# Linear attention and SwiGLU on one core: chunks 0 and 1 as pairs of batches, tiled attention, eight PSUM banks in turn

## The chip, the core and the metric

The kernel runs on one core of a Trainium2 chip. The metric is the device time of one execution in microseconds (us). Three executions of the kernel before took 251.66, 251.06 and 250.78 us; their median is 251.06 us. Six units matter here: PE (TensorE, matmuls), DVE (VectorE), ACT (ScalarE), POOL (GpSimd[...]), SP (SyncE, which only issues DMAs here) and the DMA engines.

## What is computed

The inputs are q, k and v of shape (4 batches, 8 heads, 768 tokens, 64), two weight matrices of 512 x 1536, one of 1536 x 512, and a vector of 512. First comes a linear attention with a decay for each head, then an RMS norm over the 512 numbers of a token, then a SwiGLU network:

```python
for t in range(S):
    state = gamma[None, :, None, None] * state + np.einsum('bhd,bhe->bhde', k[:, :, t], v[:, :, t])
    y[:, :, t] = scale * np.einsum('bhd,bhde->bhe', q[:, :, t], state)
x = np.ascontiguousarray(y.transpose(0, 2, 1, 3)).reshape(B * S, H * D)
xn = x / np.sqrt(np.mean(x * x, axis=-1, keepdims=True) + 1e-06) * rms_g
g = xn @ w_gate
return (g / (1.0 + np.exp(-g)) * (xn @ w_val)) @ w_out
```

Both kernels take the 768 tokens in six chunks of 128. Within a chunk y is a masked (q k^T) v plus q times the state of the chunks before; then the state gains k^T v. The decay is folded into scales: v is multiplied by gamma^-position and y by gamma^position.

## The kernel before

A chunk has four units, one for each batch: 128 tokens on 128 partitions. For each chunk the network (`ffn`) then runs over all four batches together, 512 tokens wide. It has twelve `gv` steps (eight 128x512 matmuls each, one SiLU on ACT, one product hT on DVE) and a `down` for each batch (twelve 128x512 matmuls, one copy on ACT, one store). Chunk c's network is the outer loop, and the attention of chunk c+1 is laid between its steps by tables of slots (PLAN for chunks 2 to 5, PLAN1 for chunk 1). The schedule is manual: each engine executes its instructions in the order in which the code issues them, and waits where it needs another engine's result or a buffer.

A unit of attention has these pieces. `piece_t` transposes q and k on PE (chunks 0 and 1 only; from chunk 2 on a DMA issued on SP does it, in `cast`). `piece_a` computes a = k q^T for 8 heads into two PSUM tiles (eight matmuls that use 64 rows of the array each) and masks them on DVE (am, line 219). `piece_y` has eight matmuls am v (line 232), four with the state (line 237), four for k^T v (line 244), then on DVE the scaled copy x (line 247) and the state's sum st_f (line 259), on ACT the squares (line 251), on POOL mean and power (lines 272 and 275). `piece_n` scales x to xn, and `piece_x` (chunks 0 and 1) or a DMA turns xn over into xnT, which the network reads.

Chunk 0 has nothing to hide behind. A string of steps orders its four batches (line 384: C cast, T transpose, V scaled v, A, Y, W a quarter of the gate and value weights, N, X, S), and the network of chunk 0 starts when all four are done, after five matmuls whose result is not used (`warm_up`).

Loads: chunk 0's first batch and chunks 1 to 5 come as float32 by SP, in runs of 64 numbers (256 bytes), and POOL casts q and k to bf16 and scales v (lines 178 to 181). Batches 1 to 3 of chunk 0 and all weights come by POOL's queue, cast on the way.

PSUM has eight banks. Four belong to the pool `aps` (attention), four to `fps` (network, and chunk 0's k^T v); each pool hands out its four in turn.

```python
    aps = ctx.enter_context(tc.tile_pool(name="aps", bufs=4, space=bass.MemoryType.PSUM))
    fps = ctx.enter_context(tc.tile_pool(name="fps", bufs=4, space=bass.MemoryType.PSUM))
    PLAN = dict(cast=(0, 1, 2, 3), t=(1, 3, 5, 7), a=(4, 6, 8, 10), y=(6, 8, 10, 12), n=(8, 10, 12, 13), x=(8, 10, 12, 14))
```

Of the kernel before, what the change touches and what calls it, by code (L numbers as in the profile page):

```python
# [11 lines left out]
AX = mybir.AxisListType  # L12
# [5 lines left out]
def kernel(  # L18
# [11 lines left out]
    nc = tc.nc  # L30
# [15 lines left out]
    loads = ctx.enter_context(tc.tile_pool(name="loads", bufs=8))  # L46
    work = ctx.enter_context(tc.tile_pool(name="work", bufs=3))
    ffw = ctx.enter_context(tc.tile_pool(name="ffw", bufs=3))
    aps = ctx.enter_context(tc.tile_pool(name="aps", bufs=4, space=bass.MemoryType.PSUM))
    fps = ctx.enter_context(tc.tile_pool(name="fps", bufs=4, space=bass.MemoryType.PSUM))  # L50


    out_v = out.rearrange("(b c p) m -> c b p m", b=B, p=C)

    SYNC_DEP = mybir.DependencyInfo(mybir.DependencyClass.Sync, mybir.DependencyReason.DATA)


    raw = {}

    def load(c, b, after=None):  # L60
        t = []
        for name, src in (("q_f", q), ("k_f", k), ("v_f", v)):
            x = loads.tile([128, H, D], F32, name=name)
            i = nc.sync.dma_start(
                out=x, in_=src[b].rearrange("h (c p) d -> c p h d", p=C)[c])
            if after is not None:
                tc.add_manual_dep(i.ins, after.ins.name, SYNC_DEP, reason="transfer order")
            t.append(x)
        raw[c, b] = t

    raw0 = {}

    def load0(b):
        for name, src in (("qb", q), ("kb", k)):
            x = work.tile([128, DM], BF16, name=name, bufs=6)
            nc.gpsimd.dma_start(
                out=x.rearrange("p (h d) -> p h d", h=H),
                in_=src[b].rearrange("h (c p) d -> c p h d", p=C)[0])  # L80
            raw0[name, b] = x
        x = loads.tile([128, H, D], F32, name="v_f")
        nc.gpsimd.dma_start(out=x, in_=v[b].rearrange("h (c p) d -> c p h d", p=C)[0])
        raw0["v", b] = x

    load(0, 0)
    g_col = const.tile([128, KS], F32, name="g_col")
    with nc.allow_non_contiguous_dma(reason="one column per 128 entries"):
        nc.scalar.dma_start(out=g_col, in_=moe_rms_g.rearrange("(s p) -> p s", p=128))


    pos_i = const.tile([128, NCH], mybir.dt.int32, name="pos_i")
    nc.gpsimd.iota(pos_i, pattern=[[C, NCH]], base=1, channel_multiplier=1)

    lngs = const.tile([128, H], F32, name="lngs")
    for h in range(H):
# [5 lines left out]
    pos_f = const.tile([128, NCH], F32, name="pos_f")  # L102
    nc.vector.tensor_copy(pos_f, pos_i)
    darg = const.tile([128, NCH, H], F32, name="darg")
    nc.vector.tensor_tensor(
        out=darg, in0=pos_f[:, :, None].to_broadcast([128, NCH, H]),
        in1=lngs[:, None, :].to_broadcast([128, NCH, H]), op=ALU.mult)
    vdec = const.tile([128, NCH, H], F32, name="vdec")
    ydec = const.tile([128, NCH, H], F32, name="ydec")
    nc.scalar.activation(vdec, darg, AF.Exp, scale=-1.0, bias=zero)  # L110
    nc.scalar.activation(ydec, darg, AF.Exp, scale=1.0, bias=lnscale)

    warm = const.tile([128, 1], F32, name="warm")
    nc.scalar.activation(warm, zero, AF.Silu)
    mhalf = const.tile([128, 1], F32, name="mhalf")
    nc.vector.memset(mhalf, -0.5)
    ident = const.tile([128, 128], BF16, name="ident")
    make_identity(nc, ident)
    causal = const.tile([128, 128], BF16, name="causal")
    nc.gpsimd.memset(causal, 1.0)  # L120
    nc.gpsimd.affine_select(
        out=causal, in_=causal, compare_op=ALU.is_ge, fill=0.0, base=0,
        pattern=[[1, 128]], channel_multiplier=-1)
    for b in range(1, B):
        load0(b)

    g_bc = const.tile([128, DM], F32, name="g_bc")

    st_f = [const.tile([128, NHP, 2 * D], F32, name=f"st_f{b}") for b in range(B)]
    st_b = [const.tile([128, NHP, 2 * D], BF16, name=f"st_b{b}") for b in range(B)]
    for b in range(B):
        nc.vector.memset(st_b[b], 0.0)


    wg_b = const.tile([128, KS, DFF], BF16, name="wg_b")
    wv_b = const.tile([128, KS, DFF], BF16, name="wv_b")
    wo_b = const.tile([128, NFF, DM], BF16, name="wo_b")
    wg_v = moe_w_gate.rearrange("(k p) n -> p k n", p=128)  # L140
    wv_v = moe_w_val.rearrange("(k p) n -> p k n", p=128)
    wo_v = moe_w_out.rearrange("(n p) m -> p n m", p=128)
    WB = 384

    landed = {}

    def load_w(i):
        sl = slice(i * WB, (i + 1) * WB)
        nc.gpsimd.dma_start(out=wg_b[:, :, sl], in_=wg_v[:, :, sl])
        landed["w", i] = nc.gpsimd.dma_start(out=wv_b[:, :, sl], in_=wv_v[:, :, sl])  # L150

    def load_wo(i):
        sl = slice(i * 4, (i + 1) * 4)
        landed["wo", i] = nc.gpsimd.dma_start(out=wo_b[:, sl, :], in_=wo_v[:, sl, :])
# [296 lines left out]
```

## Time and profile before

| what | value |
|---|---|
| median of three executions | 251.06 us |
| span of the profiled execution, first to last instruction | 248.7 us |
| PE busy | 225.9 us, 91% of the span |
| DVE, ACT, POOL busy | 128.1, 87.4, 95.2 us |
| granted PE clock, mean | 0.993 |
| moved by DMA | 35.94 MB |
| DMA share in the 40 slices | near 90% or over in the first 15, little from slice 30 on |

The page gives busy times of each engine, and what ended its idle times. A busy PE says that matmuls were in flight; how fast they went is read from the distance of their starts. The median of the executions lies 2.4 us above the profiled span: that is time before the first and after the last instruction, or the difference of one execution from another.

### The profile page before, as it was taken

The page shows a single profiled execution, that of the slowest core. Times are in us where ns is not written, and L with a number is a line of the kernel's source. Part 1 is how long each engine was busy: PE and PEld are TensorE (multiplying, and loading weights), DVE is VectorE, ACT ScalarE, POOL GpSimd, SP SyncE. Part 2 cuts the span into 40 slices and gives each one's busy share as a digit, 9 for nine tenths or more (in the row PEclk, how much of TensorE's full clock was granted, in tenths as well). Part 3 has the DMA queues.
Part 4 walks back from the last instruction along what each step waited for, and adds up shares of the span by engine and source line. Part 5 has one row for each costly group of instructions (what it writes and reads, how often), then busy time and mean ns, then how long its engine had stood idle before and what let it go on. Part 6 is the DMA issues. An engine that isn't in the chain of part 4 may idle for free.

```text
span 248.7 us, 4121 instructions
## 1 busy us (share of the span) xinstructions
PE 225.9 (91%) x1495; PEld 114.4 (46%) x1521; DVE 128.1 (51%) x215; ACT 87.4 (35%) x170; POOL 95.2 (38%) x177
## 2 busy tenths in 40 slices
PE   1776999979996989999989999989999999999993
PEld 0553445545433545445544445544444444444443
DVE  4796337676234895036894046894047781134300
ACT  6365334531431242232342322433232422332221
POOL 8978144953850236910246910246900211000000
PEclk9997999999999999999999999999999999999999
DMA  9999999898997699955999356999453114200022
GB/s 140 174 195 203 196 219 221 151 199 167 218 290 109 144 222 189 229 127 87 213 209 175 127 131 98 199 207 209 122 115 66 21 21 129 86 0 0 0 87 86
DMA packets 108213, 35.94 MB, mean 145 GB/s; under 512 B 99040, under 2 KB 104928, under 8 KB 108192
## 3 DMA queue, kind: packets, MB, share of 16 engines
q1 hardware_dynamic: 95232, 29.24, 60.8%
q0 software_dynamic: 12288, 6.29, 19.0%
q8 instruction: 12, 0.20, 0.3%
q10 hardware_dynamic: 672, 0.13, 0.3%
q14 instruction: 9, 0.07, 0.1%
HBM read 28.58 MB, written 6.29 MB: 140 GB/s over the span
## 4 chain that ended last, share of the span: by engine, by line
PE 77%; DVE 10%; DMA 5%; issue 3%; ACT 3%; POOL 0%; SPq 0%; DVEq 0%; ACTq 0%
PE o_ps L361 24%; PE v_ps L338 21%; PE g_ps L335 21%; DVE am L219 4%; PE a_ps L215 3%; PE y_ps L232 2%; DMA v_f<-in_v_dram 2%; DVE x L247 2%; DMA k_f<-in_k_dram 2%; PE kv_ps L244 1%; PE y_ps L237 1%; DMA kT<-kb 1%; DVE xn L283 1%; PE o_ps L351 1%; PE qk_ps L199 1%
## 5 line engine op out<-in xcount | busy, mean ns | idle before, releaser
L341 DVE TENSOR_TENSOR hT<-sg,v_ps 128x512 bf16<-128x512 bf16 x72 | 49.4, 687 | 89.6 <-PE v_ps L338 83.2
L338 PE MATMUL v_ps<-xnT,wv_b 128*128 128x512 bf16 x282 | 73.4, 379 | 0.5
L335 PE MATMUL g_ps<-xnT,wg_b 128*128 128x512 bf16 x276 | 72.9, 380 | 0.4
L340 ACT ACTIVATE sg<-g_ps 128x512 bf16<-128x512 f32 x72 | 42.8, 594 | 63.7 <-PE g_ps L335 62.2
L361 PE MATMUL o_ps<-wo_b,hT 128*128 128x512 bf16 x269 | 60.8, 379 | 1.2 <-DMA wo_b<-in_moe_w_out_dram 0.8
L338 PEld LDWEIGHTS <-wv_b 128*128 128x128 bf16 x288 | 28.2, 98 | 34.0
L335 PEld LDWEIGHTS <-wg_b 128*128 128x128 bf16 x288 | 26.6, 98 | 31.5 <-issue 0.9
L361 PEld LDWEIGHTS <-hT 128*128 128x128 bf16 x276 | 26.6, 98 | 30.9 <-issue 0.8
L272 POOL TENSOR_SCALAR ms<-ssq 128x1 f32<-128x1 f32 x24 | 4.5, 189 | 92.4 <-ACT xsq L251 92.3
L251 ACT ACTIVATE xsq<-x 128x512 f32<-128x512 f32 x24 | 15.1, 630 | 48.7 <-DVE x L247 48.6
L219 DVE TENSOR_TENSOR am<-a_ps,causal 128x512 bf16<-128x512 f32 x48 | 30.8, 682 | 2.4 <-PE a_ps L215 2.4
L366 ACT COPY o_sb<-o_ps 128x512 f32<-128x512 f32 x23 | 13.5, 585 | 36.8 <-PE o_ps L361 30.7
L180 POOL TENSOR_TENSOR vp<-v_f,vdec 128x512 bf16<-128x512 f32 x20 | 20.7, 1037 | 3.4 <-DMA v_f<-in_v_dram 3.4
L268 POOL CAST st_b<-st_f 64x256 bf16<-64x256 f32 x40 | 17.3, 432 | 1.3
L247 DVE TENSOR_TENSOR x<-y_ps,ydec 128x512 f32<-128x512 f32 x24 | 16.4, 685 | 1.4 <-PE y_ps L237 0.8
L232 PE MATMUL y_ps<-vp,am 128*128 128x64 bf16 x192 | 12.0, 200 | 5.4 <-DVE am L219 5.1
L178 POOL CAST qb<-q_f 128x512 bf16<-128x512 f32 x20 | 12.1, 606 | 8.7 <-DMA q_f<-in_q_dram 7.9
L283 DVE SCALAR_TENSOR_TENSOR xn<-x,rstd,g_bc 128x512 bf16<-128x512 f32 x16 | 12.5, 784 | 5.5 <-POOL rstd L275 5.5
L232 PEld LDWEIGHTS <-am 128*128 128x128 bf16 x192 | 9.2, 101 | 13.1 <-DVE am L219 9.7
L275 POOL TENSOR_TENSOR rstd<-ms,mhalf 128x1 f32<-128x1 f32 x24 | 13.2, 552 | 2.0
L179 POOL CAST kb<-k_f 128x512 bf16<-128x512 f32 x20 | 12.2, 609 | 2.6 <-DMA k_f<-in_k_dram 1.7
L259 DVE TENSOR_TENSOR st_f<-st_f,kv_ps 128x512 f32<-128x512 f32 x16 | 10.8, 676 | 0.0
(60 smaller groups left out, 125.5 us busy)
## 6 DMA issues: line engine op xcount, KB each, us to landing
out_dram<-o_sb SPq DMA_DIRECT2D x23, 256.0 KB, 2.2
q_f<-in_q_dram SPq DMA_DIRECT2D x21, 256.0 KB, 4.8
k_f<-in_k_dram SPq DMA_DIRECT2D x21, 256.0 KB, 5.0
v_f<-in_v_dram SPq DMA_DIRECT2D x21, 256.0 KB, 5.1
wg_b<-in_moe_w_gate_dram POOLq DMA_DIRECT2D x4, 384.0 KB, 9.6
wv_b<-in_moe_w_val_dram POOLq DMA_DIRECT2D x4, 384.0 KB, 10.7
wo_b<-in_moe_w_out_dram POOLq DMA_DIRECT2D x3, 512.0 KB, 8.3
v_f<-in_v_dram POOLq DMA_DIRECT2D x3, 256.0 KB, 6.2
```

What stands on the lines that cost most here:

```text
L180: nc.gpsimd.tensor_tensor(out=vp, in0=v_f, in1=vdec[:, c, :, None].to_broadcast([128, H, D]), op=ALU.mult)
L219: nc.vector.tensor_tensor(out=am[:, i], in0=a_ps[i], in1=causal[:, None, :].to_broadcast([128, NHP, 128]), op=ALU.mult)
L232: nc.tensor.matmul(y_ps[:, h, :], d["am"][:, i, hp, :], d["vp"][:, h, :], start=first, stop=last, skip_group_check=True)
L247: nc.vector.tensor_tensor(out=x, in0=y_ps, in1=ydec[:, c, :, None].to_broadcast([128, H, D]), op=ALU.mult)
L251: nc.scalar.activation(xsq, x.rearrange("p h d -> p (h d)"), AF.Square, accum_out=ssq)
L268: nc.gpsimd.tensor_copy(st_b[b][r, :, i * 64:i * 64 + 64], st_f[b][r, :, i * 64:i * 64 + 64])
L283: nc.vector.scalar_tensor_tensor(out=xn, in0=x, scalar=d["rstd"], in1=g_bc, op0=ALU.mult, op1=ALU.mult)
L335: nc.tensor.matmul(g_ps, wg_b[:, s, sl], xnT[:, s, :], start=s == 0, stop=s == KS - 1)
L338: nc.tensor.matmul(v_ps, wv_b[:, s, sl], xnT[:, s, :], start=s == 0, stop=s == KS - 1)
L340: nc.scalar.activation(sg, g_ps, AF.Silu)
L341: nc.vector.tensor_tensor(out=hT[:, n, :], in0=sg, in1=v_ps, op=ALU.mult)
L361: nc.tensor.matmul(o_ps, hT[:, n, b * C:(b + 1) * C], wo_b[:, n, :], start=n == 0, stop=n == NFF - 1)
```

## The change

The body of the kernel is written anew; the arithmetic is the same.

- **Chunks 0 and 1 in pairs.** A unit is now a pair of batches: 64 partitions for each of two batches, two neighbouring tokens on a partition (e = 0, 1), loaded by `load_pair` in runs of 128 numbers (512 bytes). The pieces for a pair are `tp` (transposes), `ap` and `ap_mask`, `y0` or `y1`, `kvp`, and they use quarters or halves of the array. Chunk 0's decay goes into float32 masks (`mask_exp`), so that v needs only a cast, and y no scaling; its statistics are taken from PSUM, and its state comes later, from `vp_pair` on POOL and `kvp` on PE.
- **The network from two batches on.** Chunk 0's `gv` steps for feature blocks 0 to 4 run 256 tokens wide on the first pair, then on the second; blocks 5 to 11 run 512 wide. Chunk 1 does blocks 0 to 5 in halves.
- **One attention phase a pair** for chunks 2 to 5 (`phase`): a for the next pair, then y with the state, k^T v, and am v for two batches. The state is kept as 64 x 64 blocks, so that the state and k^T v matmuls are half as wide and use half the array each.
- **Eight PSUM tiles of one bank in turn** (`bank`), for everything.
- **Loads by POOL's queue**, q and k cast on the way; SP keeps the first pair's q and v and the second's v of chunk 0, and the transposing DMAs. POOL no longer casts q and k. Stores go from SP to ACT, but for the last half tile.
- Seven matmuls (`heat`) run at the start, and the SiLU table is loaded on ACT at the first SiLU instead of at the start.

The diff, cut to its core (the constants, the other pieces and most of the hand-written order are left out):

```diff
--- before.py
+++ after.py
-    loads = ctx.enter_context(tc.tile_pool(name="loads", bufs=8))
-    aps = ctx.enter_context(tc.tile_pool(name="aps", bufs=4, space=bass.MemoryType.PSUM))
-    fps = ctx.enter_context(tc.tile_pool(name="fps", bufs=4, space=bass.MemoryType.PSUM))
+    psum = ctx.enter_context(tc.tile_pool(name="psum", bufs=1, space=bass.MemoryType.PSUM))
...
+    pair_v = {n: s.rearrange("b h (c j e) d -> c b j h (e d)", c=NCH, e=2) for n, s in srcs.items()}
...
+    def bank(name, dtype=F32):
+        i = turn[0] % 8
+        turn[0] += 1
+        return psum.tile([128, 512 if dtype == F32 else 1024], dtype, name=name, tag=f"p{i}")
...
+    def load_pair(c, p, n, eng=None, f32=False, after=None):
+        u = U.setdefault((c, p), {})
+        if n == "v" or f32:
+            x = work.tile([128, H, 2 * D], F32, name=n + "2f", tag="x" if n == "q" else "v2f", bufs=2)
+        else:
+            x = work.tile([128, H, 2 * D], BF16, name=n + "2b", bufs=3)
+        for b in range(2):
+            i = (eng or nc.gpsimd).dma_start(out=x[b * 64:b * 64 + 64], in_=pair_v[n][c, 2 * p + b])
+            if after is not None:
+                tc.add_manual_dep(i.ins, after.ins.name, SYNC_DEP, reason="transfer order")
+        u[n] = x
...
+    def mask_exp(a):
+        for i in range(2):
+            for x in range(2):
+                nc.scalar.activation(mask0[a][i][:, x], reach, AF.Exp, scale=lng[2 * (2 * a + x) + i], bias=lnscale)
...
+    def heat(n):
+        hot = bank("hot")
+        for _ in range(n):
+            nc.tensor.matmul(hot, ones[:, :128], ones, start=True, stop=True)
...
+    def tp(c, p, n, a, eng):
+
+        u = U[c, p]
+        ps = bank("t_ps", BF16)
+        view = ps[:, :512].rearrange("p (x b e j) -> p x e b j", x=2, b=2, e=2)
+        for x in range(2):
+            for e in range(2):
+                for i in range(2):
+                    h = 2 * (2 * a + x) + i
+                    nc.tensor.transpose(view[i * 64:i * 64 + 64, x, e], u[n][:, h, e * D:e * D + D], ident)
+        t = work.tile([128, 2, 2, 2, 64], BF16, name=n + "2T", tag=n + "T", bufs=8)
+        copy(eng, t.rearrange("p x b e j -> p (x b e j)"), ps[:, :512])
+        u[n + "T", a] = t
...
+    def ap(c, p, a):
+        u = U[c, p]
+        qt, kt = u["qT", a], u["kT", a]
+        ps = [bank("a_ps") for _ in range(2)]
+        for x in range(2):
+            for e in range(2):
+                o = (x * 2 + e) * 128
+                for b in range(2):
+                    for i in range(2):
+                        r, t = slice(i * 64, i * 64 + 64), slice(b * 64, b * 64 + 64)
+                        nc.tensor.matmul(ps[i][t, o:o + 128], kt[r, x, b, e], qt[r, x, b], start=True, stop=True)
...
+        am = work.tile([128, 2, 2, 128], BF16, name="am2", tag="am", bufs=12)
+        m = mask0[a][i] if c == 0 else causal_p[:, None, :].to_broadcast([128, 2, 256])
+        last_mask[0] = nc.vector.tensor_tensor(
+            out=am.rearrange("p x e t -> p x (e t)"),
+            in0=u["a_ps", a][i].rearrange("p (x t) -> p x t", x=2), in1=m, op=ALU.mult)
...
+    def vp_pair(c, p):
+        u = U[c, p]
+        x = work.tile([128, H * 2, D], BF16, name="vp2", bufs=3)
+        nc.gpsimd.tensor_tensor(
+            out=x, in0=u["v"].rearrange("p h (e d) -> p (h e) d", e=2),
+            in1=vd_p[:, c].rearrange("p h e -> p (h e)")[:, :, None].to_broadcast([128, 2 * H, D]), op=ALU.mult)
...
+    def y0(p, a):
+        for x in range(2):
+            for i in range(2):
+                h = 2 * (2 * a + x) + i
+                for e in range(2):
+                    for b in range(2):
+                        r = slice(b * 64, b * 64 + 64)
+                        nc.tensor.matmul(u["y"][b][:, h * D:h * D + D], u["am", a, i][r, x, e, :],
+                                         u["vb"][r, h, e * D:e * D + D],
+                                         start=h == 0 and e == 0, stop=h == H - 1 and e == 1, skip_group_check=True)
...
+    def kvp(c, p):
+        for hp in range(NHP):
+            for e in range(2):
+                for b in range(2):
+                    for i in range(2):
+                        r, t = slice(b * 64, b * 64 + 64), slice(i * 64, i * 64 + 64)
+                        s = slice(e * D, e * D + D)
+                        h = 2 * hp + i
+                        nc.tensor.matmul(u["kv"][b][t, hp * D:hp * D + D], u["k"][r, h, s], u["vp"][r, h, s],
+                                         start=hp == 0 and e == 0, stop=hp == NHP - 1 and e == 1,
+                                         skip_group_check=True)
...
+    def state_diag(p):
+        for i in range(2):
+            r = slice(i * 64, i * 64 + 64)
+            nc.gpsimd.tensor_copy(st_d[p][r, :, :, i * D:i * D + D], st_f[p][r])
+
+    def state_cast(p):
+        nc.gpsimd.tensor_copy(st_b[p], st_f[p])
...
+        u = pair(c, p)
+        r = work.tile([128, 2], F32, name="rstd", bufs=4)
+        nc.gpsimd.tensor_tensor(out=r, in0=u["ms"], in1=mhalf, op=ALU.pow)
+        u["rstd"] = r
...
+    def y1(p):
+        u = U[1, p]
+        u["y"] = [bank("y_ps") for _ in range(2)]
+        for b in range(2):
+            for hp in range(NHP):
+                nc.tensor.matmul(u["y"][b][:, hp * 128:(hp + 1) * 128],
+                                 u["qT", hp // 2][:, hp % 2, b].rearrange("p e j -> p (e j)"), st_d[p][:, b, hp],
+                                 start=hp == 0, stop=False, skip_group_check=True)
...
+                    nc.tensor.matmul(u["y"][b][:, h * D:h * D + D], u["am", hp // 2, i][r, hp % 2, e, :],
+                                     u["vp"][r, h, e * D:e * D + D], start=False,
+                                     stop=h == H - 1 and e == 1, skip_group_check=True)
...
+    def phase(c, p, nxt=None):
+
+        u = U.setdefault((c, p, "pair"), {})
+        bs = (2 * p, 2 * p + 1)
+        if nxt is not None:
+            for j in range(2):
+                a_pe(nxt[0], 2 * nxt[1] + j)
+        ys = [bank("y_ps") for _ in range(2)]
+        for j, b in enumerate(bs):
+            for hp in range(NHP):
+                for i in range(2):
+                    r = slice(i * 64, i * 64 + 64)
+                    o = j * 256 + hp * D
+                    nc.tensor.matmul(ys[i][:, o:o + D], U[c, b]["qT"][r, hp, :], st_b[p][r, j, hp, :],
+                                     start=j == 0 and hp == 0, stop=False, skip_group_check=True)
+        if c < NCH - 1:
+            kv = bank("kv_ps")
+                        nc.tensor.matmul(kv[i * 64:i * 64 + 64, o:o + D], U[c, b]["k"][:, h * D:h * D + D],
+                                         U[c, b]["vp"][:, h, :], start=True, stop=True)
+                    nc.tensor.matmul(ys[i][:, o:o + D], U[c, b]["am"][i][:, hp, :], U[c, b]["vp"][:, 2 * hp + i, :],
+                                     start=False, stop=j == 1 and hp == NHP - 1, skip_group_check=True)
+        u["y"] = ys
...
+    def gv(c, n0, n1, t0, t1):
+        m = (n1 - n0) * w
+        ps = []
+        for wt, name in ((wg_b, "g_ps"), (wv_b, "v_ps")):
+            x = bank(name)
+            for n in range(n0, n1):
+                o = (n - n0) * w
+                for s in range(KS):
+                    nc.tensor.matmul(x[:, o:o + w], wt[:, s, n * 128:(n + 1) * 128], XT[c][:, s, t0:t1],
+                                     start=s == 0, stop=s == KS - 1)
...
+    def down(c, b):
+        ps = bank("o_ps")
+        for n in range(NFF):
+            nc.tensor.matmul(ps, HT[c][:, n, b * C:(b + 1) * C], wo_b[:, n, :], start=n == 0, stop=n == NFF - 1)
+        o_sb = work.tile([128, DM], F32, name="o_sb", bufs=3)
+        nc.scalar.copy(o_sb, ps)
+        store(nc.scalar, c, b, slice(0, DM), o_sb)
...
-    for step in ("C0 T0 V0 W0 A0 T1 V1 Y0 W1 A1 T2 V2 Y1 W2 N0 A2 T3 X0 V3 Y2 W3 S0 N1 A3 S1 X1 Y3 N2 X2 S2").split():
-        P[step[0]](0, int(step[1]))
...
+    begin(0)
+    heat(7)
+    load_pair(0, 0, "v", nc.sync, after=late_i)
+    load_pair(0, 1, "q")
+    load_pair(0, 1, "k")
+    load_w(0, 1)
+    places()
+    exponents()
+    load_w(1, 2)
...
+    load_pair(0, 1, "v", nc.sync, after=last_mask[0])
+    v_cast(0)
+    decays()
+    tp(0, 1, "q", 0, "a")
+    y0(0, 0)
+    tp(0, 1, "q", 1, "v")
+    y0(0, 1)
...
+    tp(0, 1, "k", 1, "a")
+    eps0(0)
+    power(0, 0)
+    ap(0, 1, 0)
+    ap(0, 1, 1)
+    norm0(0)
+    load_w(2, 3)
+    load_w(3, 5)
...
+    x_copy(0, 0, 0, "v")
+    x_copy(0, 0, 1, "a")
+    ap_mask(0, 1, 0, 0)
+    v_cast(1)
+    gv(0, 0, 1, 0, 256)
+    ap_mask(0, 1, 0, 1)
+    load_w(5, 8)
+    gv(0, 1, 2, 0, 256)
+    y0(1, 0)
+    y0(1, 1)
+    squares0(1)
+    eps0(1)
+    power(0, 1)
+    vp_pair(0, 0)
+    for p in range(2):
+        nc.gpsimd.memset(st_d[p], 0.0)
+    gv(0, 2, 3, 0, 256)
+    norm0(1)
...
+    gv(0, 4, 5, 0, 256)
+    kvp(0, 0)
+    state0(0, "a")
+    for n in "qkv":
+        load_pair(1, 0, n)
+    load_w(8, 10)
+    load_w(10, 12)
+    gv(0, 0, 2, 256, 512)
+    vp_pair(0, 1)
+    state_diag(0)
+    gv(0, 2, 4, 256, 512)
+    gv(0, 4, 5, 256, 512)
+    kvp(0, 1)
+    state0(1, "a")
...
+    for i in range(3):
+        load_wo(4 * i, 4 * i + 4)
+    gv(0, 5, 6, 0, GT)
+    state_diag(1)
+    vp_pair(1, 0)
...
+    load(2, 2)
+    load(2, 3)
+    down(0, 3)
...
+    y1(1)
+    y1_out(1)
+    squares(1, 1)
...
+                0: [L(begin, d)],
+                2: [L(phase, d, 0, (d, 1)), L(a_mask, d, 2)] + [L(load, d + 1, 2), L(t_dma, d + 1, 0), L(t_dma, d + 1, 1)] * more,
+                3: [L(a_mask, d, 3)],
+                4: [L(y_out, d, 0), L(squares, d, 0)],
+                5: [L(state_add, d, 0)] * more + [L(load, d + 1, 3)] * more,
...
+                8: [L(phase, d, 1, (d + 1, 0) if more else None)]
+                   + [L(a_mask, d + 1, 0), L(t_dma, d + 1, 2), L(t_dma, d + 1, 3)] * more,
+                9: [L(a_mask, d + 1, 1)] * more,
+                10: [L(y_out, d, 1), L(squares, d, 1)],
...
```

## The prediction

> **What bounds the kernel now.** I read the busy table by stage first, cut where each chunk's network starts (the first `g_ps` of a chunk in PE's timeline: 24.38, 65.43, 104.53, 141.29, 178.26, 213.61 us), because a mean over the span hides that the stages differ.
>
> ```profile
> core 0: us, PE busy (x) PEld busy (x) DVE busy (x) ACT busy (x) POOL busy (x), PEclk, DMA share, GB/s
> 0.00:24.38 24.38, 14.11 (x133) 9.44 (x135) 17.09 (x42) 14.04 (x30) 20.38 (x39) 0.93 1.38 178
> 24.38:65.43 41.05, 38.80 (x285) 20.20 (x288) 22.54 (x36) 15.22 (x27) 21.58 (x40) 1.00 1.10 194
> 65.43:104.53 39.10, 35.74 (x237) 17.62 (x240) 20.58 (x32) 12.05 (x24) 18.34 (x33) 1.00 1.04 200
> 104.53:141.29 36.76, 35.63 (x236) 17.64 (x240) 20.49 (x32) 12.05 (x24) 14.78 (x29) 1.00 0.88 162
> 213.61:244.86 31.25, 31.09 (x154) 15.13 (x155) 8.25 (x12) 9.88 (x17) 0.00 (x0) 1.00 0.09 34
> ```
>
> The first 24.4 us have no network: a chain over DVE, PE, ACT and POOL. The last chunk is network alone: 144 matmuls of 512 columns in 31.25 us, 0.216 us each, and PE never waits. So six chunks cost at least 187 us; what a stage takes above 31.1 us is attention and waits. Then PE's and DVE's timelines inside chunk 1, two separate answers:
>
> ```profile
> 78.57 1.03 PE L335 MATMUL g_ps<-xnT,wg_b 128*128 128x512 bf16 x4
> 79.44 1.03 PE L338 MATMUL v_ps<-xnT,wv_b 128*128 128x512 bf16 x4
> 80.30 0.40 PE L232 MATMUL y_ps<-vp,am 128*128 128x64 bf16 x8
> 80.53 0.39 PE L237 MATMUL y_ps<-st_b,qT 128*128 128x128 bf16 x4
> 80.76 0.39 PE L244 MATMUL kv_ps<-vp,kb 128*128 128x128 bf16 x4
> 81.08 0.40 PE L215 MATMUL a_ps<-qT,kT 64*128 64x128 bf16 x8
> 81.41 1.04 PE L335 MATMUL g_ps<-xnT,wg_b 128*128 128x512 bf16 x3
> ```
>
> ```profile
> 80.57 0.69 DVE L341 TENSOR_TENSOR hT<-sg,v_ps 128x512 bf16<-128x512 bf16 x1 [1.04 <-PE v_ps L338]
> 81.17 0.68 DVE L247 TENSOR_TENSOR x<-y_ps,ydec 128x512 f32<-128x512 f32 x1
> 81.78 0.68 DVE L259 TENSOR_TENSOR st_f<-st_f,kv_ps 128x512 f32<-128x512 f32 x1
> 82.37 0.69 DVE L219 TENSOR_TENSOR am<-a_ps,causal 128x512 bf16<-128x512 f32 x1
> ```
>
> The starts in the first say what attention costs PE: 0.23 (y), 0.23 (state), 0.32 (kv), 0.33 (a), 1.11 us a batch. The second says that hT begins 0.27 us after PE is free of its `v_ps` (80.30), and that DVE then starts one operation each 0.60 us. POOL's timeline, last:
>
> ```profile
> 10.09 0.83 POOL L149 DMA_DIRECT2D wg_b<-in_moe_w_gate_dram  x1
> 10.83 0.83 POOL L150 DMA_DIRECT2D wv_b<-in_moe_w_val_dram  x1
> 12.09 0.19 POOL L272 TENSOR_SCALAR ms<-ssq 128x1 f32<-128x1 f32 x1 [0.43 <-ACT xsq L251]
> 12.36 0.57 POOL L275 TENSOR_TENSOR rstd<-ms,mhalf 128x1 f32<-128x1 f32 x1
> ```
>
> A DMA issue holds POOL for 0.75 to 0.95 us (nine unit loads and eight weight loads in the first 21 us), and what stands behind it waits.
>
> **What the Trainium skill says.** "TensorE: Matmul & The Clock Gate", Part 3: matmuls in different tiles of the array run together. The trace agrees: eight half-height a matmuls (L215) take the 0.40 us of four full ones. "TensorEngine Tiling (Array Packing)", Key Properties: a change of tiling mode drains the array. Agreed: kv to a is 0.32 us where four matmuls need 0.23, so 0.09 a change. The same page, Restrictions: column tiling switches fast weight load off; before has no column tiling, so no run shows it. "ScalarE: Activation LUTs", What ACT_TABLE_LOAD costs, gives 1283 ns; both loads of before show 1.28 us.
>
> **The change, step by step.**
>
> *Start, up to the first network step.* The q pair (512 KB on SP) should land near 4.9 us (before: 256 KB at 4.25, 512 KB at 5.45). Two DVE casts (0.90 each) end at 6.8; transposes, copies (0.43) and the spread of g to 9.4. k comes by POOL behind three iotas, issued from 2.1; POOL's loads took 5.4 to 6.2 us to land, so near 8.2. Its transposes run after g's copies; second copy on ACT at 10.6. `mask_exp(1)` (four exps, 0.37 each) then ends at 12.2. Four masks on DVE end at 13.3; the v cast (1.0 on ACT) at 13.2; four small exps (0.33) and a copy to 15.1. y0 ends near 14.5, squares at 15.9, power (0.55 on POOL) at 17.3, xn at 18.1, eight transposes and the copies at 19.4. So the network starts near 19.5 instead of 24.38: 4.9 us earlier, but on two batches.
>
> *Second pair.* ACT casts v (1.0) and only now loads the SiLU table (1.28), so the first hT is done near 22.7. On DVE three of the pair's four masks stand behind that hT: last mask at 24.6. PE idles about 3 us here. y0, squares (0.82) and power follow: power ends at 27.2. Half of the first ten half-steps (4.3 us of PE) hides in this.
>
> *A new queue on POOL.* Behind that power stand, in order, `vp_pair(0,0)` (two L180 of 1.04: 2.1), two memsets (0.2 for 128 columns, 0.5 to 0.9 for 1024; I take 0.5 each), ten DMA issues (six of `load_pair(1,0)`, four of weights; 0.78: 7.8), and `vp_pair(0,1)` (2.1): 27.2 + 13.1 = 40.3 us. PE needs that last tile for `kvp(0,1)` after xn (0.9), transposes (0.5), one half-step (0.9), `kvp(0,0)` (0.35) and five more half-steps (4.3): 34.2 us. PE waits some 6 us; everything behind on PE waits with it. Bounds: 3 (issues at 0.6, quick memsets) to 7.5 us.
>
> *Rest of chunk 0.* From 40.3: `kvp(0,1)` 0.35; seven full gv steps 12.1; downs 10.4 (48 of 0.216); chunk 1's attention, two pairs of tp (32 transposes in halves: 16 steps of 56 ns, 0.9), ap (four quarters together: 0.45 + 0.1), kvp (0.23 to 0.45 for half-width; 0.35 + 0.1), y1 (0.45 + 0.45 + 0.2), and one pair's x (0.45): 6.5. Sum 69.6. After a 6 us pause PE runs at half clock for a window; before shows 0.5 to 0.6 from 21 to 25 us after its thin stretch. I add 0.8: 70.4 us against 65.43, **+5.0**.
>
> *Chunks 1 to 4.* A phase costs PE 0.45 (a) + 0.23 (state, in halves) + 0.3 (kv, 0.23 to 0.45) + 0.46 (16 am v) + 0.3 (three or four mode changes) = 1.75 us for two batches, before 2.22. SP's wait for POOL casts goes; chunk 1 lost 2.3 us on a k transpose (the wait list's "PE a_ps L215 <- DMA kT<-kb").
>
> *A new wait: the turn of banks.* After a phase the banks come round while DVE still holds them. Fourth bank behind the phase's start: a gv step's `v_ps` takes the bank of the third a tile, whose mask is the first DVE operation behind the hT of the step before. That mask is done 0.27 + 0.60 + 0.69 = 1.56 us after PE ended that step; PE gets there after 0.86 (its four g matmuls). It waits 0.7 us. The same geometry comes at y's first bank (y_out behind the next hT) and at kv's (state_add behind the one after): three waits a phase, two where a down stands in place of the last, one or two at c = 4. In all 3 + 5 + 5 + 2 = 15 waits, 10.5 us. Before has separate banks for attention, and its PE shows no such wait. Bounds: 0.2 each (if DVE is quicker or releases sooner) to 0.9.
>
> | stage | sum, us | before | difference |
> |---|---|---|---|
> | start and chunk 0 | 70.4 | 65.43 | +5.0 |
> | chunk 1 | 31.2 + x 0.45 + its wait for norm 1.6 + two a 0.65 + 3.5 + 2.1 = 39.5 | 39.10 | +0.4 |
> | chunk 2 | 31.1 + 3.5 + 3.5 = 38.1 | 36.76 | +1.3 |
> | chunk 3 | 38.1 | 36.97 | +1.1 |
> | chunk 4 | 31.1 + 1.35 + 0.9 + 1.4 = 34.75 | 35.35 | -0.6 |
> | chunk 5 and end | 35.1 | 35.1 | 0 |
>
> Sum +7.2 us: the span of 248.7 becomes 255.9. The median of runs stands 2.4 us above the span, and I keep that: 251.06 + 7.2 = **258.3 us**, 2.9% slower. Hidden and priced at nothing: POOL's loads from chunk 2 on (24.3 us of q and k casts go, 48 issues of 0.9, 43 us, come; POOL's 0 to 15 us a stage leave room), store issues on ACT (idle over half the time), DMA (no more bytes; longer runs for chunks 0 and 1).
>
> **The rivals.**
> - *The turn of banks costs nothing*: if PE's wait is under 0.22 us an event (7.2/15 = 0.48 less than my 0.7), the kernel is not slower. At zero: 258.3 - 10.5 = 247.8 us. For it: DVE has 14 us free in a stage. Against: the order above is fixed, and hT's 0.27 and 0.60 are measured.
> - *POOL's queue hides* (power earlier, quicker issues): 258.3 - 6 = 252.3. With both: 241.8.
> - *Column tiling is dear*: without fast weight load each of 480 column-tiled matmuls (128 tp, 128 ap, 128 kvp, 96 kv) takes 28 ns more: +13.4, 271.7 us. Against: different tiles may load weights together.
>
> **Chances.** The forecast 0.57 (own range 253 to 264), banks free 0.17, POOL hidden 0.08, both 0.06, column tiling dear 0.12. Range 244 to 266: it leaves out "both" and the far part of the dear case. Within 0.3% (0.75 us, about what a measurement can tell here) only the edges of the bank and POOL cases fall: 0.05. Faster: 0.17 + 0.06, less those edges, 0.21. Slower 0.74.
>
> **What would show it.** First gv matmul near 19.5 us; a PE wait of about 6 us before `kvp(0,1)` put down to POOL's vp; one SiLU table load near 21 us; the first 512-wide gv of chunk 1 near 70 us; waits of `v_ps` on DVE's am, x and st_f, some 0.7 us each, 15 in all; stages 2 and 3 near 38 us. I am wrong if PE reaches chunk 1 before 66 us, or if stages 2 and 3 take under 36 us.

## The result, and the profile after

The changed kernel takes 299.19 us (median of 4 executions, 296.31 to 299.99) against 251.36 us for the kernel before (median of 4): a ratio of 1.188, 95% interval 1.181 to 1.194. The forecast was 258.3 us, its range ended at 266 us. The sign is right, the size is off by 41 us. Some executions of a kernel run 1.5% or more slower than its others; the times below are medians without them.

The busy table of the changed kernel by stage, cut at the same points as before: the start of each chunk's network, and the end. The columns are the stretch, its length, busy time and count for each engine, granted PE clock (1.00 is full speed), DMA share (the time that all packets took, over the stretch's time on 16 DMA engines; packets of several queues overlap, so it can exceed 1), GB/s.

```profile
core 0: us, PE busy (x) PEld busy (x) DVE busy (x) ACT busy (x) POOL busy (x), PEclk, DMA share, GB/s
0.00:23.36 23.36, 15.35 (x186) 9.81 (x187) 11.09 (x36) 10.05 (x22) 13.65 (x31) 0.67 1.01 132
23.36:76.36 53.00, 45.57 (x563) 27.06 (x568) 24.94 (x49) 18.02 (x36) 39.60 (x47) 0.86 1.15 151
76.36:131.82 55.46, 38.85 (x347) 23.43 (x345) 25.95 (x39) 14.12 (x30) 25.54 (x30) 0.88 1.09 114
131.82:184.88 53.06, 37.78 (x269) 17.88 (x273) 20.49 (x30) 11.03 (x23) 23.31 (x28) 0.90 1.18 107
184.88:228.25 43.37, 37.08 (x271) 17.00 (x272) 21.31 (x30) 11.84 (x24) 13.24 (x17) 0.96 0.78 103
228.25:262.30 34.05, 33.31 (x222) 15.77 (x224) 15.36 (x24) 11.79 (x24) 1.87 (x4) 1.00 0.17 47
```

Chunks 1 and 2 stand out. PE is busy there for 38 to 39 us, little more than before, but the stages last 53 to 55 us. The DMA share is as high as before or higher, while the bytes a second fell from 200 and 162 to 114 and 107, and the whole kernel moved 30.5 MB where the kernel before moved 35.9: the transfers got dearer, not more.

| stage | forecast, us | measured | difference |
|---|---|---|---|
| start and chunk 0 | 70.4 | 76.4 | +6.0 |
| chunk 1 | 39.5 | 55.5 | +16.0 |
| chunk 2 | 38.1 | 53.1 | +15.0 |
| chunk 3 | 38.1 | 43.4 | +5.3 |
| chunk 4 | 34.75 | 34.05 | -0.7 |
| chunk 5 and end | 35.1 | 34.7 | -0.4 |

The sum, 41 us, is the whole miss (span 297.0 against 255.9). What PE waited for, from the list of waits (total, times, longest, in us):

```profile
PE x_ps L359 <- DVE xn L426: 11.7, 2, 10.8
PE a_ps L449 <- DMA kT<-kb: 8.9, 2, 5.2
PE v_ps L520 <- DVE st_f L499: 6.0, 3, 2.2
PE kv_ps L298 <- POOL vp L269: 5.7, 1, 5.7
PE o_ps L539 <- DVE st_f L499: 3.1, 2, 1.6
PE v_ps L520 <- DVE am L458: 3.0, 5, 0.6
PE v_ps L520 <- DVE x L406: 3.0, 5, 0.6
```

Lines 3, 5, 6 and 7 are the forecast's turn of banks: 3 + 2 + 5 + 5 = 15 waits, 15.1 us. Line 4 is its queue on POOL. Of the first, chunk 1's wait for the norm, the forecast had 1.6 us, and the second, the wait for kT that cost the kernel before 2.3 us, it expected to go. The first is named after DVE, but DVE had waited for POOL, and POOL for ACT. ACT's timeline at that place:

```profile
77.61 0.59 ACT L541 COPY o_sb<-o_ps 128x512 f32<-128x512 f32 x1 [5.13 <-PE g_ps L520]
84.00 3.19 ACTq L532 DMA_DIRECT2D out_dram<-o_sb  x2
87.24 0.63 ACT L416 ACTIVATE xsq<-x 128x512 bf16<-128x512 f32 x1 [9.04 <-DMA kT<-kb]
```

ACT finished the last copy of chunk 0 at 78.2 us, and then the store of that tile was not issued until 84.0 and 86.7 (two halves). The squares of chunk 1's second pair, which the norm needs, stood behind it. The brackets name the releaser: a transposing DMA of chunk 2's k, on SP's queue. The instructions of the program say how a store on ACT comes to wait for it (numbers are places in each engine's order):

```
SP  8 L440 DmaTransposeAnt qT_1208<-qb_1038 [waits DMAHW5_49,DMASW6_49,PE_49]
SP  9 L440 DmaTransposeAnt kT_1210<-kb_1040 [waits DMAHW6_49,DMASW7_49,Activation_49]
ACT 59 L532 DMACopy out_0_dram<-o_sb_1237 [waits DMAHW5_49,Activation_49]
ACT 60 L532 DMACopy out_0_dram<-o_sb_1237 [waits DMAHW6_49]
```

The DMAs of SP and ACT are given eight completion semaphores in turn, and a new one waits until the last user of its semaphore has landed. The store drew the two semaphores of batch 1's transposes. SP issued these at 74.6 and 75.9 us, and they landed 9.4 and 10.8 us later, at 84.0 and 86.7: the very times at which the two halves of the store were issued. Transposes landed late all over the kernel: here are the lines of the lists of DMAs on them (which unit issued them, how many, and last the median time in us from issue to landing), first of the kernel before, then of the changed one.

```profile
qT<-qb SPq DMA_TRANSPOSE x16, 2.4
kT<-kb SPq DMA_TRANSPOSE x16, 2.4
```

```profile
qT<-qb SPq DMA_TRANSPOSE x16, 7.2
kT<-kb SPq DMA_TRANSPOSE x16, 7.9
```

That left two theories, and the experiments were made to tell them apart. **A**: the order of issue (a store behind a transpose on ACT) is the cost. **B**: POOL's casting loads fill the DMA engines and slow the transposes, whoever issues what.

### The profile page after: what moved, and what is told of

Its sections match the earlier page's. It is cut to its first block, busy times and chain, and to the rows that moved or that the text cites. A ratio compares the mean times of both kernels' runs of the same rounds, so it can differ in the third digit from the quotient of the medians.

```text
span 297.0 us, 5024 instructions
## 1 busy us (share of the span) xinstructions
PE 239.1 (81%) x1999; PEld 126.1 (42%) x2021; DVE 127.8 (43%) x220; ACT 86.7 (29%) x175; POOL 117.2 (39%) x154
## 5 line engine op out<-in xcount | busy, mean ns | idle before, releaser
L525 DVE TENSOR_TENSOR hT<-sg,v_ps 128x512 bf16<-128x512 bf16 (+1 forms) x75 | 49.4, 665 | 129.9 <-ACT sg L524 64.5
L520 PE MATMUL v_ps<-xnT,wv_b 128*128 128x512 bf16 (+1 forms) x330 | 78.5, 366 | 13.1 <-DVE st_f L499 6.0
L520 PE MATMUL g_ps<-xnT,wg_b 128*128 128x512 bf16 (+1 forms) x319 | 78.7, 369 | 3.4 <-issue 2.2
L524 ACT ACTIVATE sg<-g_ps 128x512 bf16<-128x512 f32 (+1 forms) x75 | 42.5, 577 | 89.5 <-PE g_ps L520 88.8
L541 ACT COPY o_sb<-o_ps 128x512 f32<-128x512 f32 x23 | 13.5, 585 | 53.1 <-PE o_ps L539 40.0
L416 ACT ACTIVATE xsq<-x 128x512 bf16<-128x512 f32 x20 | 12.4, 621 | 33.0 <-DVE x L406 20.3
L458 DVE TENSOR_TENSOR am<-a_ps,causal 128x512 bf16<-128x512 f32 x32 | 20.5, 682 | 2.6 <-PE a_ps L449 2.6
L432 POOL TENSOR_TENSOR vp<-v_f,vd_n 128x512 bf16<-128x512 f32 x16 | 18.7, 1197 | 0.0
L103 POOL DMA_DIRECT2D qb<-in_q_dram x16 | 15.0, 939 | 0.0
L100 POOL DMA_DIRECT2D v_f<-in_v_dram x16 | 14.6, 914 | 0.3 <-DMA qb<-in_q_dram 0.3
L103 POOL DMA_DIRECT2D kb<-in_k_dram x16 | 14.3, 895 | 0.0
L359 PE MATMUL x_ps<-ident,xn 128*128 128x128 bf16 x32 | 3.5, 264 | 11.7 <-DVE xn L426 11.7
L406 DVE TENSOR_TENSOR x<-y_ps,yd_n 128x512 f32<-128x512 f32 x16 | 10.2, 682 | 0.0
```

The costliest lines, as they stand in the source:

```text
L100: nc.gpsimd.dma_start(out=x, in_=unit_v[n][c, b])
L103: nc.gpsimd.dma_start(out=x.rearrange("p (h d) -> p h d", h=H), in_=unit_v[n][c, b])
L406: nc.vector.tensor_tensor(out=x[:, :, :, i, :], in0=u["y"][i].rearrange("p (b a d) -> p b a d", b=2, a=NHP), in1=yd_n[:, c, i][:, None, :, ...
L416: nc.scalar.activation(xsq, u["x"][:, b], AF.Square, scale=1.0 / math.sqrt(DM), accum_out=ms[:, b:b + 1])
L432: nc.gpsimd.tensor_tensor(out=x, in0=U[c, b]["v"], in1=vd_n[:, c, :, None].to_broadcast([128, H, D]), op=ALU.mult)
L458: nc.vector.tensor_tensor(out=am, in0=u["a_ps"][i].rearrange("p (a t) -> p a t", a=NHP), in1=causal[:, None, :].to_broadcast([128, NHP, 12 ...
```

## The experiments

All start from the changed kernel. Stages are from one profiled execution each. The kernel before took 250.8 to 251.4 us beside them.

| run | us | ratio to before, 95% | start of chunk 1 | chunk 1 | chunk 2 | chunk 3 | chunk 4 |
|---|---|---|---|---|---|---|---|
| changed kernel | 299.19 | 1.181 to 1.194 | 76.4 | 55.5 | 53.1 | 43.4 | 34.1 |
| e1 stores on SP | 283.43 | 1.117 to 1.138 | 76.4 | 43.2 | 50.9 | 42.7 | 34.1 |
| e2 float32 loads by SP | 275.20 | 1.079 to 1.112 | 78.6 | 44.3 | 41.4 | 41.4 | 34.1 |
| e3 split phase | 276.32 | 1.089 to 1.111 | 74.5 | 54.0 | 40.8 | 35.7 | 33.8 |
| e4 one vp moved | 294.45 | none | 75.5 | 55.5 | 53.2 | 43.4 | 34.1 |
| e5 one store on POOL | 291.66 | 1.151 to 1.171 | 77.1 | 47.5 | 52.0 | 42.7 | 34.1 |
| e6 = e1 + e2 + e3 | 269.58 | 1.063 to 1.083 | 74.7 | 45.4 | 42.7 | 35.4 | 33.8 |
| e7 POOL relieved | 293.35 | 1.157 to 1.179 | 69.9 | 56.8 | 52.0 | 42.7 | 34.1 |
| e8 = e6 + e7 | 264.19 | 1.046 to 1.060 | 69.7 | 45.2 | 41.8 | 35.4 | 33.8 |
| e9 kT earlier | 267.29 | 1.060 to 1.070 | 74.3 | 50.1 | 37.2 | 35.4 | 33.8 |
| e10 shorter start | 265.57 | 1.054 to 1.064 | 73.8 | 48.6 | 36.9 | 35.4 | 33.8 |
| e11 SP's order | 257.64 | 1.026 to 1.033 | 67.6 | 45.9 | 38.1 | 35.4 | 33.8 |
| e12 ACT stores, late v | 261.93 | 1.031 to 1.045 | 75.4 | 39.9 | 40.8 | 36.6 | 33.8 |

**e1 and e5: who issues the stores.** e1 changes `store(nc.scalar, ...)` in `down` to `store(nc.sync, ...)`. e5 moves the store of one tile of 24:

```diff
-        store(nc.scalar, c, b, slice(0, DM), o_sb)
+        store(nc.gpsimd if (c, b) == (0, 3) else nc.scalar, c, b, slice(0, DM), o_sb)
```

> Only the queue of the output stores changes: all full-width stores are issued by SP instead of ACT. Theory A (the store of chunk 0's last batch on ACT waits for an earlier DMA of SP with which it shares a completion semaphore, and ACT's squares wait behind it): ACT's idle of 9.04 us before the first xsq of chunk 1's second pair and PE's 10.84 us before x_ps go; chunk 1's stage falls from 55.5 to 43-46 us and the span from 297 to 280-287 us. Theory B (the transposes and casting loads crowd the DMA engines, and ACT would wait for late data anyway): chunk 1's stage stays above 52 us and the span above 293 us.

> One store alone changes: that of chunk 0's last batch is issued by POOL, which is idle there, instead of ACT; every load, transpose and other store stays where it is. Theory A (in that store ACT waits for a transpose that shares its semaphore, and PE waits for ACT): PE's 10.84 us before x_ps shrink to 1-2 us, chunk 1's stage goes from 55.5 to 43-45 us, chunk 2's stays within 50-54 us, span 284-287 us. Theory B (DMA engines too full, the order of issue doesn't matter in chunk 1): chunk 1's stage stays above 52 us.

e1: chunk 1 fell by 12.3 us and its wait before `x_ps` to 1.8 us in two pieces; chunk 2 fell by 2.1 only. e5, where every load and transpose is as it was, shows in chunk 1, in the list of PE's waits there:

```profile
PE x_ps L359 <- DVE xn L426: 2.3, 2, 1.2
PE a_ps L449 <- DMA kT<-kb: 1.9, 1, 1.9
```

11.7 us of wait became 2.3. In chunk 1 theory A holds. The stage fell by 8.0 us, not by the 10.5 to 12.5 expected, because PE, now earlier, met the late kT (second line). Chunk 2 kept 8.2 us of waits for kT: there A explains nothing.

**e2: the loads.** q, k and v from chunk 2 on come as float32 on SP's queue, as in the kernel before, and POOL casts q and k ahead of the transposes:

```diff
-                nc.gpsimd.dma_start(out=x.rearrange("p (h d) -> p h d", h=H), in_=unit_v[n][c, b])
+                nc.sync.dma_start(out=x.rearrange("p (h d) -> p h d", h=H), in_=unit_v[n][c, b])
...
+            x = work.tile([128, DM], BF16, name=n + "b", bufs=5)
+            nc.gpsimd.tensor_copy(x, u[n])
```

> q, k and v from chunk 2 on are loaded as float32 by SP's queue and q and k cast on POOL just ahead of their transposes, as the kernel before did; stores stay on ACT. Theory A (order behind shared semaphores, whatever the load): chunk 1's wait before x_ps stays at 8-11 us, the span falls by less than 5 us. Theory B (casting loads cost the DMA engines 2 us a tensor where plain ones of before cost 1.2, and slow the transposes that run beside them): landings of qT and kT fall from a median of 7.2-7.9 to 2.5-4 us, PE's waits for kT in chunk 2 (8.9 us) and most of the 10.84 us in chunk 1 go, and the span falls to 275-282 us.

The median landings of the transposes, from e2's list of DMAs, and its busy table for chunks 1 to 3:

```profile
qT<-qb SPq DMA_TRANSPOSE x16, 2.6
kT<-kb SPq DMA_TRANSPOSE x16, 2.5
```

```profile
78.62:122.93 44.31, 36.80 (x351) 22.19 (x346) 25.93 (x39) 13.63 (x29) 20.08 (x28) 1.00 0.77 154
122.93:164.31 41.38, 35.55 (x272) 16.54 (x273) 20.28 (x30) 11.25 (x23) 14.50 (x21) 1.00 0.83 162
164.31:205.69 41.38, 35.55 (x273) 16.58 (x272) 20.18 (x30) 11.84 (x24) 12.11 (x17) 1.00 0.61 129
```

The transposes are as quick as before, no wait for kT is left in any stage (2.5 us for xnT, at the start of chunk 2, are new), and the PE clock is full again (0.88 and 0.90 before this edit). The stall of chunk 1 is gone although the stores still are on ACT, and although e2 moves more bytes (34.7 MB against 30.5). So the two theories are two links of one chain: the casting loads make the transposes late (B), and the store on ACT passes that lateness on to the norm of chunk 1 (A); in chunk 2 PE meets the late kT itself. What e2 doesn't separate is the cast from the queue: float32 loads on SP stand in one queue with the transposes, and don't run beside them. Which of the two slowed the transposes more stays open.

The packets of the trace give the sizes. In the changed kernel from 64 to 90 us a load of q or k is 1024 packets of 128 bytes at 35 ns, over 16 engines 2.2 us; before, 1024 packets of 256 bytes at 18 to 25 ns, 1.2 to 1.6 us. The price goes with the cast and not with POOL's queue: v, which the same queue loads without a cast, took 64 packets of 4096 bytes at 262 ns in the same stretch, 1.0 us a tensor. (These are estimates: a packet's time can hold some waiting for other packets.) The transposes' 256-byte packets took 49 ns on average while loads ran (64 to 88 us), and 19 ns at 88 to 92 us, when none did. That they share engines is stated by the Trainium skill: "DMA: Bandwidth & Descriptors", Issuing engines are not separate DMA queues, has DMAs of all three issuers run on the same 16 engines and interleave. What that costs, only the runs here show. The same page, Anatomy of one DMA, says that a wait of a DMA for a semaphore is made by the issuing sequencer: ACT's 5.8 us before 84.0 are one.

**e3: the turn of banks.** The phase is cut in three, with masks and `y_out` directly behind their matmuls; from chunk 3 on:

```diff
-                2: [L(phase, d, 0, (d, 1)), L(a_mask, d, 2)] + ...
-                3: [L(a_mask, d, 3)],
-                4: [L(y_out, d, 0), L(squares, d, 0)],
-                5: [L(state_add, d, 0)] * more + ...
+                1: [L(a_pe, d, 2), L(a_mask, d, 2)],
+                2: [L(phase, d, 0), L(y_out, d, 0), L(squares, d, 0)] + ...
+                3: [L(state_add, d, 0)] * more,
+                4: [L(a_pe, d, 3), L(a_mask, d, 3)],
```

> From chunk 2 on the attention phase is issued in three pieces in separate steps: the a matmuls of one batch at a time with their masks directly behind, then y and kv with y_out behind it, state_add one step later. The banks that return to the network's g_ps and v_ps were then read at least one step earlier. If the turn of the banks is what stops PE there, the waits of v_ps and o_ps on DVE (15.1 us in all) fall under 4 us and the span falls by 10-13 us, to 284-287 us. If they only cover time that PE would lose to late transposes, the span falls by less than 4 us. Chunk 1's wait before x_ps should stay as it is (10-11 us).

Of the fifteen waits two are left, 0.7 us together; the span fell by 23.5 us, more than expected. The busy table of e3 for chunks 2 and 3:

```profile
128.42:169.23 40.81, 38.81 (x273) 17.95 (x274) 20.59 (x30) 11.61 (x24) 19.02 (x22) 0.92 1.17 129
169.23:204.94 35.71, 35.55 (x273) 16.67 (x272) 20.18 (x30) 11.72 (x24) 13.07 (x16) 1.00 0.80 120
```

Chunk 3 is the clean reading: PE waits for next to nothing, and the stage takes 35.7 us instead of 43.4. In chunk 2 the edit also asks for kT later, so that the waits for it shrink from 8.9 to 0.3 us; its gain of 12.3 us is not the banks' alone. e6 and e2 differ in chunk 3 by the split (and the stores): 41.4 against 35.4, 6.0 us for 5.8 us of bank waits.

**e4 and e7: POOL's queue in chunk 0.** e4 moves `vp_pair(0, 1)` ahead of the memsets and the ten issues. e7 takes work off POOL: three scalings of v go to DVE, the copies into the doubled state to ACT, v of chunk 1 is loaded by SP, the memsets go into an idle stretch.

> On POOL the scaling of the second pair's v moves ahead of two memsets and ten DMA issues. PE's 5.71 us before kv_ps of the second pair go; chunk 1's network starts 5-6 us earlier (70.5-71.5 instead of 76.4 us) if nothing else is late; loads of chunk 1 and of the last weights come 2 us later. The span falls by 4-6 us. If chunk 1's loads or the weights decide in its place, a new wait of 2-5 us stands at t_ps or g_ps in chunk 0 and the span falls by under 2 us.

> Three of the four scalings of v of chunks 0 and 1 go from POOL to DVE, the copies into the doubled state to ACT, two memsets into POOL's idle time, and v of chunk 1 is loaded by SP. If POOL's whole queue between 31 and 51 us is what chunk 0 waits for (moving one item in it turned 5.7 us of wait into 4.2 us at the next item), both waits of kv_ps on POOL go, chunk 0's network takes 46.5-49 us instead of 53.0 and the span falls by 4-7 us, to 290-293 us. If the loads of chunk 1 are late whatever POOL does, a wait of t_ps for k2b of 2 us or more takes their place and the span falls by under 3 us. Chunk 1's stall of 10.8 us stays.

In e4 the wait of `kvp(0, 1)` went and the next product of the same queue made PE wait instead; PE's timeline:

```profile
51.34 0.64 PE L298 MATMUL kv_ps<-vp,k2b 64*64 64x64 bf16 x32 [4.24 <-POOL vp L269]
```

That is `kvp(1, 0)`, behind `vp_pair(1, 0)` at 49.4 us, where the queue ends as it did without the edit. Chunk 1 started only 0.8 us earlier (the profile is of the longer of e4's two executions, 298.87 us, so only its waits are read). e7 removed both waits: chunk 0's network took 46.65 us instead of 53.0. A queue that is full is not shortened by putting its items in another order.

**e6 and e8: together.**

> Stores on SP, float32 loads by SP with casts on POOL, and the split phase together, start and chunk 0 untouched. If the three are separate costs: start and chunk 0 76-79 us, chunk 1 40-42, chunk 2 35.5-37, chunk 3 35.5-36, chunk 4 33.8, chunk 5 and end 34.7: span 256-263 us, and what is left over the kernel before stands in start and chunk 0 alone. If the split phase gained in chunk 2 only by asking for kT later, chunk 2 with the three together takes no less than 40 us.

> The three of e6 and POOL's relief together. If all act on separate stretches: 70-73 us to the start of chunk 1's network, the rest as in e6, span 250-257 us, the same as or up to 3 per cent slower than the kernel before. The later chunks then gain some 3 us on the kernel before (phase of two batches), start and chunk 0 still lose 5-7 us.

Chunks 3 and 4 came as expected. Both miss in chunks 1 and 2, where e6 waits 9.4 and e8 8.9 us for kT again (e6's expectation had named this case: chunk 2 not under 40 us if e3 had gained there only by asking later; it took 42.7). SP now holds loads, transposes and stores, and in its order the transposes of one chunk's second half stand behind the loads of the next chunk.

**e9 to e12: SP's order and the start.** e9 asks for chunk 2's loads earlier (8 us were intended) and puts transposes ahead of later loads. e10 adds to it a start with g loaded by two transfers instead of spread by PE, the SiLU table loaded after the first xn, and one v cast on POOL. e11 is e8 with that start and only the transposes moved up. e12 puts the stores back on ACT, one load behind the transposes of xn, and the first v behind the casts of q.

> e8 with the loads of chunk 2 issued some 8 us earlier and the transposes of batches 2 and 3 of chunks 2 and 3 ahead of the next chunk's loads in SP's order; nothing else. If the two waits for kT that e8 keeps (3.9 us in chunk 1, 5.0 us in chunk 2) are only a matter of SP's order, both go: chunk 1 from 45.2 to 40-41.5 us, chunk 2 from 41.8 to 35.5-37 us, span 250-253 us, within 2 per cent of the kernel before. If the DMA engines are too full there, the waits move to the next loads or to vp, and the span stays above 257 us.

> e9 with a shorter start: g comes by two small transfers on ACT's queue instead of ten float32 matmuls between the transposes of q and k, the SiLU table is loaded in an idle stretch of ACT before the first network step, and the second pair's v is cast on POOL. If those matmuls (3.7 us of PE ahead of k's transposes) and the table load (1.28 us, with 1.05 us of cast, ahead of the first sg) are what made the start 3.9 us longer than forecast: the network starts at 20-21.5 us instead of 23.2, chunk 1's at 65.5-67.5 instead of 69.7 us, span 246-250 us, within 1 per cent of the kernel before. If k's data decides the start, less than 1.5 us is gained.

> e8 with the shorter start of e10, and with only SP's order changed after it: the transposes of chunk 2's batches 2 and 3 stand ahead of chunk 3's loads, and each later chunk's first two transposes ahead of the load of its third batch; the loads of chunk 2 stay where e8 has them. If the waits for kT in e8 (3.9 us in chunk 1, 5.0 us in chunk 2) are SP's order, chunk 1 takes 40-42 us and chunk 2 36-39 us, chunk 1 starts at 67.5-68.5 us and the span is 247-252 us, within 1 per cent of the kernel before. If the DMA engines are too full whatever the order, the waits move to xnT or vp as in e9 and the span stays above 256 us.

> e11 with three changes in two places. In the start the first pair's v is loaded after q is cast, so that k's transfer has the DMA engines: k's transposes start 1-2.5 us earlier (e11 waits 3.0 us for k2b) and so does all behind them; chunk 1 starts at 65-67 instead of 67.6 us. Around chunk 1's end SP is relieved: stores are issued by ACT again, and one load stands behind the transposes of xn instead of ahead of them. If SP's issue queue is what e11's 5.5 us wait ahead of chunk 2 comes from, that wait falls under 3 us and chunk 1 takes 41.5-43.5 instead of 45.9 us; span 247-252 us. If stores on ACT wait again for DMAs of SP (shared completion semaphores), ACT's silu is late, waits of v_ps or hT appear at the chunks' ends and chunks 2 and 3 take over 39 us.

e9 was no gain on e8: the waits for kT went, but 8.6 us for xnT at the start of chunk 2 and 3.9 us for wo_b (1.5 in e8) came. The first load of chunk 2 was issued at 38.0 us instead of 60.4: in e8 it stood behind chunk 0's first store in SP's order, and the move took it past that store, 22 us and not 8. So it ran beside the last weights (wo_b, issued from 37.8 to 40.6 us). That the transposes of xn lost their turn on SP to the loads is the likely cause of the other wait, not shown by a run of its own. e10: the first network step came at 22.2 us, where e9 has 22.4 and e8 23.2, so the matmuls for g were next to no cost: k's transposes, rid of them, wait 2.1 us for k's data. Table and cast gave 0.7 us: from the first step to `kvp(0, 0)` 9.4 us instead of 10.0 in e8. e11 is the best version: no wait for kT over 0.4 us, but this line is new, at the first matmul of chunk 2:

```profile
PE g_ps L521 <- ACT o_sb L542: 5.5, 1, 5.5
```

ACT's copy had long been done. The matmul reads xnT, whose second pair's transposes SP issued at 109.6 us, behind three loads (105.6 to 107.9) and a store. e12 agrees, though it makes two moves at once: chunk 1 took 39.9 us, with 0.5 us left for xnT. But with the stores off SP the loads of chunk 2 were early again (39.7 us, 58.3 in e11) and wo_b made PE wait 4.2 us (1.1 in e11); ACT's stores waited for semaphores again (one was issued 2.7 us after its copy had ended and a silu was held up by 4.1 us; chunk 2, with 3.1 us of waits for kT, took 40.8); and y0 waited 5.4 us for the late v, where it had waited 1.3.

No run beat the kernel before; e11 stays 2.6 to 3.3% behind. Its chunks 3 and 4 take 35.4 and 33.8 us against 37.0 and 35.4, so these two chunks gain 1.6 us each. That fits the phase for two batches once its waits are gone, but banks, loads and stores differ too: that phase inside the kernel before was not tried. What e11 lacks lies ahead: 2.2 us in the start and chunk 0, 6.8 in chunk 1, 1.3 in chunk 2.

## Why the prediction was wrong

- **The step that failed** is the last line of the sum: "Hidden and priced at nothing: POOL's loads from chunk 2 on ..., store issues on ACT (idle over half the time), DMA (no more bytes ...)". The loads cost time not by POOL's issues nor by their bytes, but on the DMA engines: beside them the transposes landed in 7.2 to 7.9 us instead of 2.4. Whether by their 128-byte packets or by running beside the transposes at all stays open, since e2 ended both. The stores cost not by ACT's time to issue, but by what a store waits for while it heads ACT's queue: ACT stood 5.8 us and PE 10.8 us in chunk 1, and e5, by moving one store, took 8.0 us off the stage. e2 took 22 us off the span, 11.2 in chunk 1, 11.7 in chunk 2. The prediction had asked of the other steps what they are queued behind, but not of these.
- **A term of the right mechanism, too small**: the turn of banks. Fifteen waits were forecast and fifteen came, but that the count fits is luck: by chunk 3, 5, 5 and 2 were forecast for chunks 1 to 4, and 3, 6, 6 and none came, since the downs waited as well. The ten on am and x took 0.6 us each (forecast 0.7), the five behind `state_add` 1.5 to 2.2, 15.1 us in all instead of 10.5. The rival "banks free" falls with e3. The forecast let the hT ahead of that addition wait for PE alone; at such a place it waited for ACT, whose SiLU (sg) stood behind two squares of x, while DVE stood idle for 2.2 us (lines of the three engines' timelines, in order of time):

```profile
198.55 0.63 ACT L416 ACTIVATE xsq<-x 128x512 bf16<-128x512 f32 x1 [3.38 <-DVE x L406]
199.18 0.61 ACT L416 ACTIVATE xsq<-x 128x512 bf16<-128x512 f32 x1
199.79 1.06 ACT L524 ACTIVATE sg<-g_ps 128x512 bf16<-128x512 f32 x2
200.40 0.69 DVE L525 TENSOR_TENSOR hT<-sg,v_ps 128x512 bf16<-128x512 bf16 x1 [2.24 <-ACT sg L524]
201.00 0.68 DVE L499 TENSOR_TENSOR st_f<-st_f,kv_ps 128x512 f32<-128x512 f32 x1
201.74 1.38 PE L520 MATMUL v_ps<-xnT,wv_b 128*128 128x512 bf16 x4 [2.21 <-DVE st_f L499]
```

- **Start**: the first network step at 23.36 us, not 19.5. q's cast began at 6.1, and k's data, forecast for 8.2, came at 10.0 in e10, whose transposes stood waiting for them for 2.1 us; the float32 matmuls for g (3.7 us of PE between the transposes of q and k) lie beside that wait.
- **POOL's queue**: `kvp(0, 1)` at 44.4 us, its wait 5.7 us where 6 were forecast: right, and late by the start's delay. That its next item would wait as well, had it been cured alone, e4 showed.
- **Column tiling dear** falls: 32 matmuls of 64 x 64 in quarters start within 0.38 us, and the phase for two batches takes PE 1.6 us, where 1.75 were forecast.
- **Half clock**: 0.8 us were allowed for one window. The granted clock stood at 0.5 for 6.8, 13.7 and 10.2 us after or within the long waits of chunks 0, 1 and 2 (stage means 0.86 to 0.90), so a lost stretch was paid again in part: after `kvp(0, 1)` at 44.4 us it stayed at 0.5 until 48.7, an estimated 2.1 us lost (half of 4.3). It was at 0.5 through the start as well, from 7.7 to 31.6 us, where the kernel before shows it from 21.2 to 24.6 only; the forecast had nothing for that. At 92.7 us eight 256-wide matmuls took 1.7 us instead of 0.87.

## What to carry to other kernels

When a transfer changes its queue or its form, price it as a task on the DMA engines (packets times time a packet) and list what now runs beside it; equal bytes are not equal time. An engine with idle time is not free to issue DMAs: whatever its DMA waits for, the compute behind it waits for as well. A pool of tiles taken in turn needs its readers ahead of the turn, and moving one item in a full queue only renames the wait. In an order written by hand, a move is worth what stands between the old place and the new: past one store, a load came 22 us earlier and not 8.

## What the runs showed of the hardware

- A casting load of q or k took the DMA engines an estimated 2.2 us (1024 packets of 128 bytes at 35 ns), a plain one in the kernel before 1.2 to 1.6 us (1024 of 256 bytes at 18 to 25 ns). A plain load of v on the queue of the casting ones took 1.0 us (64 of 4096 bytes at 262 ns).
- A store on ACT was issued at the very times, 84.0 and 86.7 us, when two transposes on SP's queue with which it shares completion semaphores had landed.
- Transposing DMAs landed in 7.2 to 7.9 us (median) beside casting loads of POOL's queue in the changed kernel, and in 4.0 to 8.8 us in the other runs with such loads (e1, e3, e4, e5, e7); where plain loads and transposes share SP's queue they landed in 2.4 us (before) and 2.5 to 3.4 us (e2, e6, e8 to e12).
- Column-tiled matmuls of 64 x 64 in the four quarters started every 12 ns on average (32 in 0.38 us); nothing like a dearer weight load shows.
